# A three-stage kernel (attention, dense layer, eight experts): the third token block is loaded at item 74, the raw weight pieces 4 to 7 use two buffers, and the logits of three blocks come one step later

## The chip, the cores and the metric

The kernel runs on one core of a Trainium2 chip (trn2). The metric is the device time of one launch in microseconds (us), lower is better. Before the change three runs gave 1095.99, 1098.74 and 1099.82 us, with a median of 1098.74 us.

## The reference

Three layers follow one another on 2304 tokens with 512 features (4 batches of 576):

```
scores = q k^T / 8 + bias(positions)          # 4 batches, 8 heads, 576 x 576, head size 64
x = softmax(scores) v                         # -> (2304, 512)
h = x @ w_in                                  # 512 -> 2048
y = (h * clip(h + 3, 0, 6) / 6) @ w_out       # 2048 -> 512
e = argmax(y @ w_gate)                        # one of 8 experts per token
out = softmax(y @ w_gate)[e] * sigmoid(y @ w_output_gate)[e] * (relu(y @ w1[e]) @ w2[e])
```

The weights `w_in` and `w_out` come in double precision and are split on the chip into two single-precision parts, so that each product of the dense layer takes three matmuls.

## The kernel before

**Attention** (class `Attn`) works off 80 items in one software-pipelined loop (`emit`, variable `s`). An item is one pair of heads of one half batch and one chunk of 128 or 64 query rows. Finished rows of x are written, transposed, to the DRAM buffer `xT_d` (L380). At fixed items the loop also calls side work of the dense layer (`early`, added to `side[s]`).

**The dense layer** (class `Moe`) takes the tokens in nine blocks (`b` = 0 to 8) of 256 tokens. `x_load(b)` (L638) brings a block from `xT_d`, `x_prep(b)` splits it into a high part (ScalarE copy, L649 or L656) and a low part (VectorE, L650 or L657). A stage `g` is one pair (b, f) of the list `seq`, where f counts 16 slices of the hidden layer: `l1_` issues 12 matmuls into one PSUM bank `ph` (L671), ScalarE makes `r` = relu(ph + 3) (L677), VectorE `t` (L678), ScalarE the high part of `g` (L680), VectorE its low part (L683); three stages later `l2_` issues 6 matmuls with them (L701). The first round of 48 stages works on blocks 0, 1 and 2 together; its first six stages are (0,0), (0,1), (1,0), (1,1), (2,0), (2,1). Stages 0 and 1 are emitted inside the last attention items, stage 2 comes after all of attention.

In the first round the weights are still being converted. There are 32 **raw pieces** p of 512 KB (even p: a slice of `w_in`, odd p: one of `w_out`). `w_load` (L576) brings a piece into a buffer `V0`, `V1` or `V2`, which attention uses for its v values before; `w_a` is a ScalarE copy of half of it (L603), `w_b` a VectorE shift (L606), `w_c` two VectorE operations, the first of which reads the raw piece for the last time (L609, L610), `w_d` a ScalarE copy and a VectorE subtraction (L613, L614). Pieces 0 to 3 are converted during attention. Pieces 4 and 5 are loaded at item 77. From stage 2 on, two stages of three (and 2, 3 and 4 in a row) carry a tick: tick p runs `w_b(p+1)`, `w_d(p)`, `w_a(p+2)` between the operations of `l1_`, and then `w_c(p+1)`, which also issues the next loads:

```python
self.w_load(p, f"V{(p - 3) % 3}")       # in w_loads(n), for every p up to n
self.conv[p][2](); self.w_loads(p + 4)  # w_c(p)
```

So pieces 6 and 7 are issued behind `w_c(4)`, at item 81, into V0 and V1, and piece 8 behind `w_c(5)`.

Each engine works strictly in the order in which instructions are emitted. All loads and stores named here are issued by SyncE (SP), in one order as well, and SP too stands still at an instruction whose buffer is not free. At stage 2 the code calls `x_load(2)`, `x_prep(2)` and `w_a(5)` ahead of the stage's own work. Block 2's rows go to the buffer `e4`, which belongs to attention's softmax until the end; its two parts go to spare columns of the bias buffers.

Four PSUM banks (m0 to m3) are handed out in turn (`mix`); when block 2's sums begin (l2 of stage 4, emitted at stage 7) they take m0 and m1, and two banks are left until stage 50.

**The tail** of a block (`tail(b)`) has six steps: `s_y` copies and stores y, two `s_t` transpose its halves (L724, copied by L725), `s_l` computes the logits from the transposed y (L730), `s_lt` chooses the expert, `s_r` counts positions. For blocks 0 to 2, `s_l` is emitted in the same stage as the second transpose.

The expert layer follows.

Of the kernel before, what the change touches and what calls it, by code (L numbers as in the profile page):

```python
# [510 lines left out]
class Moe(Base):  # L511
# [122 lines left out]
    def x_load(self, b):  # L634
        if b == 0:
            self.x01 = self.tl("K1", [2, 4, 256], name="xr")
        raw = self.x01[:, b] if b < 2 else self.tl("e4", [4, 256], name="xr")
        self.nc.sync.dma_start(raw, self.xT_d[:, :, b * 256:(b + 1) * 256].rearrange("c p t -> p c t"))  # L638
        self.xs[b] = raw

# [491 lines left out]
    def w_loads(self, n):  # L1132
        while self.loaded < min(n, 32):
            p = self.loaded
            self.w_load(p, f"V{(p - 3) % 3}")
            self.loaded += 1

    def w_a(self, p):
# [12 lines left out]
    def w_c(self, p):  # L1151
        if p < 32:
            self.conv[p][2]()
            self.w_loads(p + 4)

    def w_d(self, p):
        self.conv.pop(p)[3](self.nc.vector)
# [4 lines left out]
    def early(self, N):  # L1162

        ex = {}
        add = lambda s, f: ex.setdefault(s, []).append(f)
        self.loaded, self.conv = 4, {}
        add(31, self.setup)
        add(34, self.setup2)
        for p in range(4):
            for k, f in enumerate(self.w_early(p)):  # L1170
                add(36 + 8 * p + k, f)
        gen = self.emit()
        self.first = gen
        add(73, lambda: (self.x_load(0), self.x_load(1)))
        add(N - 3, lambda: self.w_loads(6))
        add(N - 1, lambda: self.w_a(4))
        add(N, lambda: (self.x_prep(0), self.w_b(4)))
        add(N + 1, lambda: (self.w_c(4), next(gen)))
        add(N + 2, lambda: (self.x_prep(1), next(gen)))
        return ex  # L1180

    def emit(self):
# [8 lines left out]
        add = lambda g, f: at.setdefault(g, []).append(f)  # L1191
# [12 lines left out]
        def tails(b, g, steps):  # L1204
            for k, f in zip(steps, tail[b]):
                add(g + k, f)

        tails(0, 48, (1, 2, 3, 3, 4, 5))
        tails(1, 48, (6, 7, 8, 8, 9, 10))
        tails(2, 48, (2, 12, 13, 13, 14, 15))  # L1210
        for b in range(3, NB - 1):
            tails(b, 16 * (b + 1), (2, 4, 5, 6, 7, 9))
        L = 16 * (NB - 1)
# [25 lines left out]
        for g in range(G + 2):  # L1239
            if g < G:  # L1240
                if g == 2:
                    self.x_load(2)
                    self.x_prep(2)
                    self.w_a(5)
                tk = self.tick(ticks[g]) if g in ticks else ()
                self.l1_(*seq[g], between=tk[:3])
                for f in tk[3:]:
                    f()
            while done2[0] < min(G, g + 1 - (3 if g < 49 else 2)):
                self.l2_(*seq[done2[0]])  # L1250
                done2[0] += 1
            for f in at.get(g, []):
                f()
            if g < 2:
                yield
# [126 lines left out]
```

## Time and profile before

| | us |
|---|---|
| median of three runs (lowest, highest) | 1098.74 (1095.99, 1099.82) |
| the profiled execution, its own time | 1101.62 |
| its span in the trace | 1099.9 |
| TensorE (PE) busy | 1050.7 (96%) |
| VectorE (DVE) busy | 617.7 (56%) |
| ScalarE (ACT) busy | 539.5 (49%) |
| GpSimd (POOL) busy | 221.0 (20%) |

Times in the trace count from the start of the span. Attention ends near 386 us, the first round of 48 stages goes on to about 533 us. Busy time of PE is modelled from pipelined matmuls, so a PE that is shown busy all the time can still be paced by another engine. PEclk is the granted TensorE clock as a share of 2.4 GHz; 0.50 is 1.2 GHz. In brackets behind a row stands the idle time of the engine just before it and what ended it.

### The profile page before, as it was taken

The numbers are of one execution on the slowest core, as the hardware profiler recorded it, in microseconds if no ns is written. First come the engines' busy times: TensorE is split into PE (matmuls) and PEld (weight loads), VectorE is DVE, ScalarE is ACT, GpSimd is POOL, SyncE is SP. The second block draws the span as 40 slices with busy tenths as digits, with TensorE's granted clock in tenths as the row PEclk, the third lists the DMA queues.
The fourth block names the chain that finished last, engine by engine and source line by source line (L and its number), as shares of the span: only waits on it lengthen the run. The fifth ranks groups of instructions, "written<-read, shape, count | busy, mean of one in ns | idle before, by whom it ended". The sixth has DMA issues, their size and how long they took to land. (4 is left out here: it accounts for less than half of the span.)

```text
span 1099.9 us, 20984 instructions
## 1 busy us (share of the span) xinstructions
PE 1050.7 (96%) x7637; PEld 818.7 (74%) x7637; DVE 617.7 (56%) x1554; ACT 539.5 (49%) x1198; POOL 221.0 (20%) x273
## 2 busy tenths in 40 slices
PE   5999999999999979999999999999999989999996
PEld 2355556767777769988788888898887868777774
DVE  4887865667776757776454443436355624345320
ACT  4678777667776644554333333333343123354421
POOL 0132323434444300000010000001311243221111
PEclk9999999999999989999999999999999989999998
DMA  7555481323232143431102010110421265677841
GB/s 233 173 192 171 155 281 50 107 77 97 76 95 75 52 127 113 124 126 58 58 21 39 1 39 1 39 39 2 136 77 33 56 234 209 236 291 278 330 160 38
DMA packets 62192, 129.19 MB, mean 117 GB/s; under 512 B 13820, under 2 KB 35708, under 8 KB 59264
## 3 DMA queue, kind: packets, MB, share of 16 engines
q1 hardware_dynamic: 57424, 117.69, 32.3%
q0 software_dynamic: 4512, 9.49, 3.0%
q8 instruction: 62, 1.02, 0.4%
q10 hardware_dynamic: 144, 0.59, 0.3%
q14 instruction: 50, 0.41, 0.2%
HBM read 164.08 MB, written 14.65 MB: 163 GB/s over the span
## 5 line engine op out<-in xcount | busy, mean ns | idle before, releaser
L701 PE MATMUL acc<-wp,g 128*128 128x512 f32 x864 | 227.3, 398 | 2.1 <-issue 1.7
L671 PE MATMUL ph<-xh,wp 128*128 128x256 f32 x1024 | 207.3, 285 | 1.4 <-ACT y L714 1.2
L701 PEld LDWEIGHTS acc<-wp,g 128*128 128x128 f32 x864 | 154.4, 190 | 29.4 <-issue 2.1
L345 POOL TENSOR_SCALAR e<-e,st 128x576 f32<-128x576 f32 (+1 forms) x160 | 126.2, 801 | 246.0 <-DVE st L343 177.0
L671 PEld LDWEIGHTS ph<-xh,wp 128*128 128x128 f32 x1024 | 167.0, 189 | 11.0 <-issue 3.7
L328 DVE CUSTOM_DVE_ANT_0 e<-sc,bias 128x576 f32<-128x576 f32 (+1 forms) x160 | 116.4, 751 | 63.6 <-PE sc L325 60.9
L671 PE MATMUL ph<-xl,wp 128*128 128x256 f32 x512 | 144.6, 282 | 0.7 <-issue 0.4
L677 ACT ACTIVATE r<-ph,small 128x256 f32<-128x256 f32 x144 | 67.4, 468 | 128.8 <-PE ph L671 124.3
L336 ACT ACTIVATE e<-e,st 128x576 f32<-128x576 f32 (+1 forms) x160 | 123.0, 776 | 0.0
L678 DVE SCALAR_TENSOR_TENSOR t<-r,ph 128x256 f32<-128x256 f32 x144 | 60.3, 419 | 109.8 <-ACT r L677 109.7
L680 ACT ACTIVATE g<-t 128x256 fp32r<-128x256 f32 x144 | 60.2, 418 | 115.0 <-DVE t L678 114.0
L1024 PE MATMUL peh<-ws,xt 128*128 128x512 f32 x408 | 102.7, 405 | 5.1 <-PEq L1334 5.0
L325 PE MATMUL sc<-K,q 64*128 64x288 f32 (+1 forms) x640 | 103.0, 432 | 0.1
L358 PE MATMUL pt<-cst,e 128*128 128x128 f32 (+1 forms) x720 | 97.5, 268 | 2.9 <-ACT eT L361 1.8
L671 PEld LDWEIGHTS ph<-xl,wp 128*128 128x128 f32 x512 | 97.0, 189 | 4.1 <-DVE xl L657 0.5
L358 PEld LDWEIGHTS pt<-cst,e 128*128 128x128 f32 (+1 forms) x720 | 75.8, 141 | 31.7 <-issue 14.1
L775 POOL DMA_INDIRECT tab_d<-small x18 | 18.2, 1008 | 387.6 <-DVE small L773 353.0
L1024 PEld LDWEIGHTS peh<-ws,xt 128*128 128x128 f32 x408 | 76.9, 192 | 23.1 <-issue 5.7
L683 DVE SCALAR_TENSOR_TENSOR g<-t,g 128x256 fp32r<-128x256 f32 x144 | 61.1, 424 | 56.1 <-ACT g L680 56.1
L1052 PE MATMUL peo<-ws,ehh 128*128 128x512 f32 x272 | 86.1, 398 | 0.0
L373 PEld LDWEIGHTS po<-eT,V 128*64 128x64 f32 x1280 | 64.0, 138 | 24.8 <-issue 17.4
L373 PE MATMUL po<-eT,V 128*64 128x128 f32 (+1 forms) x1280 | 81.9, 271 | 0.0
(215 smaller groups left out, 1454.5 us busy)
## 6 DMA issues: line engine op xcount, KB each, us to landing
er<-in_we SPq DMA_DIRECT2D x46, 1024.0 KB
er<-in_we SPq DMA_DIRECT2D x86, 512.0 KB
xb<-in_xb SPq DMA_DIRECT2D x38, 512.0 KB
wraw<-in_wf SPq DMA_DIRECT2D x32, 512.0 KB
cv<-in_xb SPq DMA_DIRECT2D x11, 512.0 KB
K<-in_kT SPq DMA_DIRECT2D x8, 576.0 KB
xr<-xT_d SPq DMA_DIRECT2D x9, 512.0 KB
y_d<-y SPq DMA_DIRECT2D x18, 256.0 KB
```

The costliest lines, as they stand in the source:

```text
L325: nc.tensor.matmul(self.sc[i][:R, n, :288], q[d, pr, :], self.kv[u][d, pr, n * 288:(n + 1) * 288], start=True, stop=True, tile_position=(6 ...
L328: nc.vector.tensor_tensor_reduce(out=e[:R, j, :].rearrange("p (n s) -> p n s", n=2), in0=self.sc[j][:R, :, :288], in1=self.bias[c][:R, 4 * ...
L336: self.nc.scalar.activation(e[:R, j, :], e[:R, j, :], AF.Exp, scale=-1.0, bias=st[:R, j:j + 1], accum_out=st[:R, 4 + j:5 + j])
L345: nc.gpsimd.tensor_scalar(e[:R, j, :], e[:R, j, :], st[:R, 6 + j:7 + j], 1.0, op0=ALU.mult, op1=ALU.mult)
L358: nc.tensor.transpose(pt[:, i, :R], src[3 * gi + i], self.ident[:R, :R])
L373: nc.tensor.matmul(po[64 * j:64 * j + 64, :], vm[:, 2 * pr + j, kb, :], eT[:, 2 * kb + j, :], start=kb == 0, stop=False, tile_position=(0, ...
L671: nc.tensor.matmul(ph, w, x[c], start=n == 0, stop=n == 11)
L677: nc.scalar.activation(r, ph, AF.Relu, bias=self.three)
L683: nc.vector.scalar_tensor_tensor(g[:, 1], t, 1.0 / 6.0, g[:, 0].bitcast(F32), op0=ALU.mult, op1=ALU.subtract)
L701: nc.tensor.matmul(acc[t], x, w, start=f == 0 and i == 0, stop=f == 15 and i == 2)
L1024: nc.tensor.matmul(ph[:, n, :], a, w, start=c == 0 and i == 0, stop=c == 3 and i == 2)
L1052: nc.tensor.matmul(d["po"], a, w, start=f == 0 and i == 0, stop=f == 7 and i == 2)
```

## The change

The load of block 2 moves from stage 2 to item 73 (counted from 0), behind the loads of blocks 0 and 1, and goes to the buffer `cv`, whose last user before is raw piece 3 (items 60 to 64). Raw pieces 4 to 7 use V1, V2, V1, V2. `w_c(4)` and `w_c(5)` issue loads up to piece 6 and piece 7 instead of 7 and 8; from `w_c(6)` on the rule is the old one. The tails of blocks 0 to 2 are spread so that `s_l` comes one stage behind the second transpose; the tail of block 1 so begins one stage later, block 2's transposes too.

```diff
-        raw = self.x01[:, b] if b < 2 else self.tl("e4", [4, 256], name="xr")
+        raw = self.x01[:, b] if b < 2 else self.tl("cv" if b == 2 else "e4", [4, 256], name="xr")
...
-            self.w_load(p, f"V{(p - 3) % 3}")
+            self.w_load(p, f"V{({4: 1, 5: 2, 6: 1, 7: 2}.get(p, (p - 8) % 3))}")
...
-            self.w_loads(p + 4)
+            self.w_loads(p + (3 if p < 6 else 4))
...
-        add(73, lambda: (self.x_load(0), self.x_load(1)))
+        add(73, lambda: [self.x_load(b) for b in range(3)])
...
-        tails(0, 48, (1, 2, 3, 3, 4, 5))
-        tails(1, 48, (6, 7, 8, 8, 9, 10))
-        tails(2, 48, (2, 12, 13, 13, 14, 15))
+        tails(0, 48, (1, 2, 3, 4, 5, 6))
+        tails(1, 48, (7, 8, 9, 10, 11, 12))
+        tails(2, 48, (2, 13, 14, 15, 16, 17))
...
                 if g == 2:
-                    self.x_load(2)
                     self.x_prep(2)
                     self.w_a(5)
```

On SP, from item 73 to stage 2, the order before was this (`xr` with L638 are the block loads, `wraw` with L576 the raw pieces 4, 5, 6 and 7, `xT_d` with L380 the stores of attention):

```order
L638 DMA xr_4267<-xT_d 128x4x256 x2
L380 DMA xT_d<-xo_988_4246 128x2x128
L380 DMA xT_d<-xo_1009_4339 128x2x64
L576 DMA wraw_4446<-in_wf 128x1024
L576 DMA wraw_4448<-in_wf 128x1024
L380 DMA xT_d<-xo_1028_4427 128x2x128
L380 DMA xT_d<-xo_1049_4519 128x2x128
L576 DMA wraw_4625<-in_wf 128x1024
L576 DMA wraw_4627<-in_wf 128x1024
L380 DMA xT_d<-xo_1069_4606 128x2x128
L380 DMA xT_d<-xo_1092_4716 128x2x128
L638 DMA xr_4735<-xT_d 128x4x256
```

With the change the same stretch of SP reads so (the raw pieces are 4, 5, 6 and, last, 7):

```order
L638 DMA xr_4267<-xT_d 128x4x256 x2
L638 DMA xr_4270<-xT_d 128x4x256
L380 DMA xT_d<-xo_988_4246 128x2x128
L380 DMA xT_d<-xo_1010_4341 128x2x64
L576 DMA wraw_4448<-in_wf 128x1024
L576 DMA wraw_4450<-in_wf 128x1024
L380 DMA xT_d<-xo_1029_4429 128x2x128
L380 DMA xT_d<-xo_1050_4521 128x2x128
L576 DMA wraw_4627<-in_wf 128x1024
L380 DMA xT_d<-xo_1070_4608 128x2x128
L380 DMA xT_d<-xo_1092_4716 128x2x128
L576 DMA wraw_4776<-in_wf 128x1024
```

The load of block 2 has moved ahead of six stores and four raw loads, and piece 7 from ahead of the last two stores to behind them.

On PE, at the second transpose of block 0's tail (`py` is its result, `pl` the logits, `ph` and `acc` belong to the stages), the order before was this:

```order
L671 MATMUL ph_6320<-xh_6134,wp_4773 128x256
L701 MATMUL acc_6300<-wp_3714,g_6257 128x512 x6
L724 MATMUL py_6346<-cst,y_6275 128x128 x4
L730 MATMUL pl_6352<-yT_6307,small_2291 32x256 x4
L671 MATMUL ph_6358<-xh_6134,wp_4737 128x256
```

With the change it reads so:

```order
L724 MATMUL py_6346<-cst,y_6275 128x128 x4
L671 MATMUL ph_6352<-xh_6134,wp_4735 128x256
L671 MATMUL ph_6352<-xl_6135,wp_4735 128x256
L671 MATMUL ph_6352<-xh_6134,wp_4735 128x256 x2
L671 MATMUL ph_6352<-xl_6135,wp_4735 128x256
L671 MATMUL ph_6352<-xh_6134,wp_4735 128x256 x2
L671 MATMUL ph_6352<-xl_6135,wp_4735 128x256
L671 MATMUL ph_6352<-xh_6134,wp_4735 128x256 x2
L671 MATMUL ph_6352<-xl_6135,wp_4735 128x256
L671 MATMUL ph_6352<-xh_6134,wp_4735 128x256
L701 MATMUL acc_6300<-wp_4542,g_6295 128x512 x6
L730 MATMUL pl_6378<-yT_6307,small_2291 32x256 x4
```

A whole stage of 18 matmuls now stands between the transposes and the logits; blocks 1 and 2 read alike.

## Rows read from the trace of the kernel before

**Rows 1.** Busy time by stretch: us, busy (instructions) per engine, PEclk, DMA share, GB/s

```profile
390.00:400.00 10.00, 6.27 (x24) 5.01 (x23) 4.89 (x10) 4.10 (x9) 0.00 (x0) 0.66 0.32 107
...
410.00:420.00 10.00, 7.82 (x41) 6.96 (x42) 6.27 (x14) 3.94 (x9) 0.00 (x0) 0.83 0.36 105
...
420.00:535.00 115.00, 115.00 (x730) 102.91 (x729) 82.70 (x171) 56.99 (x126) 0.00 (x0) 1.00 0.30 94
535.00:580.00 45.00, 41.30 (x288) 35.13 (x287) 21.78 (x75) 15.30 (x35) 4.05 (x4) 1.00 0.15 42
```

**Rows 2.** Timeline of SP, 340 to 440 us: start, duration, engine, line, operation

```profile
346.86 1.14 SPq L638 DMA_DIRECT2D xr<-xT_d  x2
...
386.09 0.82 SPq L576 DMA_DIRECT2D wraw<-in_wf  x2
...
387.95 0.55 SPq L638 DMA_DIRECT2D xr<-xT_d  x1
```

**Rows 3.** Timeline of ACT, 386 to 406 us

```profile
386.50 0.27 ACT L378 COPY xo<-po 128x128 f32<-128x128 f32 x1 [1.34 <-PE po L375]
393.61 1.14 ACT L649 CAST wp<-xr 128x512 fp32r<-128x512 f32 x2 [6.84 <-DMA xr<-xT_d]
...
400.68 0.67 ACT L603 ACTIVATE cvc<-wraw 128x512 f32<-128x512 f32 x1
401.25 0.46 ACT L677 ACTIVATE r<-ph,small 128x256 f32<-128x256 f32 x1
...
404.37 0.67 ACT L603 ACTIVATE cva<-wraw 128x512 f32<-128x512 f32 x1
```

**Rows 4.** Timeline of DVE, 386 to 430 us and, the last row, 505 to 515 us

```profile
394.26 1.29 DVE L650 TENSOR_TENSOR wp<-xr,wp 128x512 fp32r<-128x512 f32 x2 [8.70 <-ACT wp L649]
...
398.07 0.69 DVE L609 SCALAR_TENSOR_TENSOR cvd<-wraw,cvd 128x512 int32<-128x512 int32 x1
...
401.75 0.69 DVE L609 SCALAR_TENSOR_TENSOR cvb<-wraw,cvb 128x512 int32<-128x512 int32 x1
...
403.09 0.41 DVE L678 SCALAR_TENSOR_TENSOR t<-r,ph 128x256 f32<-128x256 f32 x1
...
406.76 0.41 DVE L678 SCALAR_TENSOR_TENSOR t<-r,ph 128x256 f32<-128x256 f32 x1
...
411.71 0.42 DVE L678 SCALAR_TENSOR_TENSOR t<-r,ph 128x256 f32<-128x256 f32 x1
...
418.82 0.42 DVE L678 SCALAR_TENSOR_TENSOR t<-r,ph 128x256 f32<-128x256 f32 x1 [2.10 <-ACT r L677]
...
427.45 0.42 DVE L678 SCALAR_TENSOR_TENSOR t<-r,ph 128x256 f32<-128x256 f32 x1
...
513.78 0.42 DVE L678 SCALAR_TENSOR_TENSOR t<-r,ph 128x256 f32<-128x256 f32 x1
```

**Rows 5.** Timeline of PE, 386 to 420 us

```profile
394.28 3.44 PE L671 MATMUL ph<-wp,wp 128*128 128x256 f32 x12 [3.58 <-ACT wp L649]
...
412.18 2.10 PE L671 MATMUL ph<-wp,wp 128*128 128x256 f32 x12 [2.72 <-DVE t L678]
...
416.64 0.28 PE L671 MATMUL ph<-xh,wp 128*128 128x256 f32 x1
...
419.45 0.28 PE L671 MATMUL ph<-xh,wp 128*128 128x256 f32 x1
```

**Rows 6.** Timeline of all engines, 276 to 281 us: one early raw load and its use

```profile
275.85 0.42 SPq L576 DMA_DIRECT2D wraw<-in_wf  x1
...
279.92 0.67 ACT L603 ACTIVATE cva<-wraw 128x512 f32<-128x512 f32 x1 [0.95 <-DMA wraw<-in_wf]
```

**Rows 7.** Timeline of PE, 536 to 582 us: the logits of blocks 0, 1 and 2

```profile
543.01 0.64 PE L730 MATMUL pl<-yT,small 128*32 128x256 f32 x8 [0.78 <-DVE yT L725]
...
560.09 0.64 PE L730 MATMUL pl<-yT,small 128*32 128x256 f32 x8 [0.87 <-DVE yT L725]
...
577.24 0.64 PE L730 MATMUL pl<-yT,small 128*32 128x256 f32 x8 [0.88 <-DVE yT L725]
```

## The prediction

> **What bounds the kernel now.** I read the busy times by stretch first, to find where PE is not busy, then the timelines of SP, ACT, DVE and PE there. Between 390 and 400 us PE is busy 6.27 of 10 us at a mean clock of 0.66, between 410 and 420 us 7.82 of 10 at 0.83, and between 535 and 580 us 41.30 of 45 [rows 1]. The rest of the first round, 420 to 535 us, shows PE busy 115.00 of 115 us. The reader should not take that for a PE bound: the VectorE operation `t` of stage 12 starts at 427.45 and that of stage 42 at 513.78 [rows 4], so three stages take 86.33 / 10 = 8.63 us, while a stage of PE alone takes 419.45 - 416.64 = 2.81 us [rows 5], three of them 8.43. The first round is paced by the chain that DVE and ACT run through each stage to convert weights. What delays that chain near 390 us delays everything up to 514 us, and PE goes straight on behind it.
>
> The chain starts late. ACT copies out the last attention rows at 386.50 for 0.27 us and then stands for 6.84 us until block 2's rows have landed [rows 3]; its two casts start at 393.61, and DVE's first operation on them at 394.26 after 8.70 us of idle [rows 4]. SP shows why: the load is issued at 387.95, behind two raw pieces at 386.09 [rows 2], which had to wait for V0, attention's last v buffer. PE itself loses 3.58 us at stage 4 [rows 5], but that is less than the chain loses.
>
> A second wait follows from the first. Stage 8 of PE starts at 412.18 after 2.72 us of idle, released by the `t` of stage 7 [rows 5], which runs from 411.71 to 412.13 [rows 4]: with two banks left, stage 8 takes the bank that stage 7 has just filled. Behind that idle time the granted clock is at its lower level, 1.2 GHz, for part of 410 to 420 us [rows 1], the 12 matmuls take 2.10 us, and the `t` of stage 9 at 418.82 comes 2.10 us after DVE was ready for it [rows 4].
>
> **The change, part by part.** *The load of block 2* goes onto SP at item 73, as a third issue behind the two that take 1.14 us together at 346.86 [rows 2]: about 0.6 us of SP, far from anything that waits. Its buffer `cv` was last read in items 60 to 64, so SP does not stand still there, and block 2's tokens (512 to 767) were stored before item 50. It has 40 us to land, and ACT's casts follow the last copy of attention directly: from 393.61 to 386.50 + 0.27 = 386.77. The chain moves forward by **6.84 us**. PE's stages 2 and 3 end before that matters, since PE had finished what it could by 394.28 - 3.58 = 390.70 [rows 5].
>
> *The raw pieces.* Piece 6 goes to V1, free behind `w_c(4)`, several us before V0 is: SP is no longer stopped there, and the piece lands early. Piece 7 is new on the path. It now goes out behind the DVE read of piece 5, which ends at 398.07 + 0.69 = 398.76 [rows 4] and with the shift at 391.92. An early raw load was in use 279.92 - 275.85 = 4.07 us after its issue, with ACT waiting for it [rows 6]; so ACT can start piece 7 at 391.92 + 4.07 = 395.99, where the shifted plan has 400.68 - 6.84 = 393.84 [rows 3]. Behind it in ACT's order stands the relu of stage 4, 401.25 - 400.68 = 0.57 us later and 0.46 long [rows 3]: it ends at 397.02. DVE wants it for the `t` at 403.09 - 6.84 = 396.25 [rows 4]. The chain loses 0.77 us. Piece 8 goes out behind the read of piece 6, ending at 401.75 + 0.69 - 6.84 = 395.60 [rows 4], and can be in use at 399.67; the relu behind it ends 1.03 us later, at 400.70, and the `t` of stage 5 is due at 406.76 - 6.84 + 0.77 = 400.69 [rows 4]. So piece 8 costs nothing more. Piece 9, queued behind piece 8, is used two stages later, and from piece 10 on the distance is the old one. I take **0.8 us back**.
>
> Bounds for that: no loss if a load is usable in 3.3 us; for the upper end I take the longest wait that the trace has near here, block 2's own load with two raw pieces in front, 393.61 - 387.95 = 5.66 us [rows 2, 3]. With it piece 8's relu ends at 395.60 + 5.66 + 1.03 = 402.29 against 399.92 planned, a loss of 2.4. I take the 4.07 because the same kind of transfer, alone, is the nearest row.
>
> The Trainium skill ("DMA: Bandwidth & Descriptors", section "Anatomy of one DMA — SWDGE (gpsimd) path") gives about 2.0 us plus bytes over 436 GB/s, for loads issued by GpSimd; an estimate by that page for 512 KB is 3.2 us, by which the loss would be nil and the time 0.8 us lower. The row of this case is 0.9 us longer, and I go by the row.
>
> *The second wait* stays. PE's operations before stage 8 and stage 8 itself are both released by the chain, so they move together, the idle time stays near 2.7 us and I expect the lower clock behind it as before, with the same 2.1 us on the `t` of stage 9. If the clock did not fall, up to 2.1 us more would be won; that goes into the range, not into the sum.
>
> *The tails.* For blocks 0, 1 and 2 PE waits 0.78, 0.87 and 0.88 us for DVE's copy of the second transpose before the logits [rows 7]; that is 2.53 of the 3.70 us of PE idle between 535 and 580 us [rows 1]. A stage of 2.81 us now stands between, longer than the wait. The matmuls are the same ones; DVE has no conversion there any more (21.78 of 45 us busy [rows 1]), and buffers of the tails are taken again many stages later. **2.5 us** won; the bounds are 0 and 2.53.
>
> **The sum.** 6.84 - 0.8 + 2.5 = 8.5 us. The profiled execution took 1101.62 us by itself, so it would take 1093.1. The median of the runs is 1098.74, 2.88 us under it; I give **1090.2 us** for the median.
>
> **The rivals.**
>
> *The load waits eat most of it.* Pieces 7, 8 and 9 come in a burst and ACT stands in order at each. By the upper end the chain gains 6.84 - 2.4 = 4.4 us; if part of the tails' gain is lost too (say 1 of 2.5), 5.9 us, which is 1092.8; if all of it, 4.4 us and 1094.3. For it: block 2's load took 5.66 us with two others in front. Against it: piece 7 has no other load in front, piece 8 is ahead of 9 on the queue. Chance 0.13.
>
> *No change.* The chain's start is not what holds PE, because some other wait of the same length stands behind the load, and only the tails' 2.5 us are won: 1096.2 us. Against it: ACT's 6.84 us are put down to the load alone, and its inputs otherwise, PE's stage 2, are finished before 390.70. Chance 0.06.
>
> *Slower.* The raw loads run late for good, not for one piece. In the old distance a load has from 398.76 to 404.37, 5.61 us, until ACT wants it [rows 3, 4], and the relu behind it has 403.09 - 401.71 = 1.38 us to spare; beyond 7.0 us each of the 24 loads from piece 8 on delays the chain that paces the whole round. At 7.6 us a load, 24 x 0.6 = 14.4 us are lost against 8.5 + 0.8 = 9.3 won: 1103.8 us. It decides from a load time of about 7.4 us. Against it: 4.07 and 5.66 us, and the order of SP, which is the old one from piece 9 on. Chance 0.03.
>
> **How the numbers follow.** The forecast has 0.78; its own range runs from 1087.3 (no loss to loads and no fall of the clock: 6.84 + 2.1 + 2.5 = 11.4 us) to 1092. The stated range reaches down to 1086.5, since the three runs lie up to 2.75 us under their median, and up to 1094.0, most of the first rival. A measurement of this kernel can tell about 0.3%, 3.3 us, from no change: faster takes the forecast and the first rival, 0.91; same 0.06; slower 0.03.
>
> **What would show it.** SP: three block loads in a row near 347 us, one raw load near 379, none between it and about 392. ACT: the casts at about 386.8 with no wait on a load, then a wait of some 2 us for piece 7 and of 1 to 2 us for piece 8. DVE: `t` of stage 4 near 397.0, that of stage 12 near 421.4. PE: no wait at stage 4, still some 2.7 us at stage 8 with the lower clock behind it, and no wait for the logits of blocks 0 to 2. I am wrong if the stage-12 `t` has moved by less than 4 us, if ACT waits 4 us or more for raw pieces, or if the waits at the logits are still there or stand at another tail operation.

## The result and the profile after

| | before | after |
|---|---|---|
| median, us (lowest to highest, 5 runs each, same chip) | 1098.74 (1095.99 to 1100.15) | 1088.31 (1085.26 to 1088.48) |
| ratio of the two, 95% interval | | 0.9902 [0.9881, 0.9922] |
| the profiled execution, its own time | 1101.62 | 1088.37 |
| its span | 1099.9 | 1086.6 |

The changed kernel is faster by 10.4 us in the median and by 13.25 us between the two profiled executions. The forecast was 8.5 us. The time lies in the range that was given, near the predicted 1090.2. One execution of E6 below (1156.88 us at a granted clock of 0.849) belongs to a slower state of the core and is left out of the median there. The first part of the page of the changed kernel shows where to look: PE has fewer busy microseconds than before (1050.7), though every matmul is still there (x7637 in both). The rows by stretch below fit with fewer of them at the lower clock.

```profile
PE 1044.1 (96%) x7637; PEld 814.8 (75%) x7637; DVE 617.9 (57%) x1554; ACT 538.7 (50%) x1198; POOL 220.7 (20%) x273
```

The busy times by stretch of the changed kernel, with the columns of [rows 1]:

```profile
390.00:400.00 10.00, 9.72 (x63) 8.67 (x63) 7.65 (x16) 4.33 (x10) 0.00 (x0) 1.00 0.56 172
400.00:410.00 10.00, 6.98 (x26) 5.49 (x25) 7.23 (x15) 4.55 (x10) 0.00 (x0) 0.67 0.44 143
410.00:420.00 10.00, 10.00 (x67) 9.18 (x67) 6.40 (x13) 4.36 (x10) 0.00 (x0) 0.99 0.20 57
...
535.00:580.00 45.00, 45.00 (x317) 38.33 (x316) 24.48 (x92) 15.56 (x38) 4.21 (x4) 1.00 0.08 23
```

The hole between 390 and 400 us is gone (6.27 us busy before, 9.72 now, clock 0.66 and now 1.00). The second hole has moved forward, from 410 to 420 into 400 to 410 us, with a clock of 0.67. From 535 to 580 us PE no longer idles (41.30 before).

SP, which issues the loads, in the changed kernel between 340 and 440 us (start, duration, line, operation):

```profile
345.56 1.69 SPq L638 DMA_DIRECT2D xr<-xT_d  x3
...
377.47 0.34 SPq L576 DMA_DIRECT2D wraw<-in_wf  x1
379.93 5.93 SPq L380 DMA_DIRECT2D xT_d<-xo  x2
390.60 45.92 SPq L576 DMA_DIRECT2D wraw<-in_wf  x12
```

Three block loads go out in a row. One raw piece (6) goes out at 377.47, and none after it until piece 7 at 390.60. ACT in the same stretch:

```profile
385.21 0.27 ACT L378 COPY xo<-po 128x128 f32<-128x128 f32 x1 [1.34 <-PE po L375]
385.37 1.14 ACT L649 CAST wp<-xr 128x512 fp32r<-128x512 f32 x2
...
394.30 0.68 ACT L603 ACTIVATE cvc<-wraw 128x512 f32<-128x512 f32 x1 [1.76 <-DMA wraw<-in_wf]
396.66 0.68 ACT L603 ACTIVATE cva<-wraw 128x512 f32<-128x512 f32 x1
```

The casts follow the last copy of attention with no wait, where 6.84 us stood before [rows 3]. Piece 7 is waited for, 1.76 us; it is used 394.30 - 390.60 = 3.70 us after its issue. Piece 8, at 396.66, is not waited for. DVE, the `t` of stages 4, 8, 9, 12 and 42:

```profile
395.37 0.42 DVE L678 SCALAR_TENSOR_TENSOR t<-r,ph 128x256 f32<-128x256 f32 x1 [0.44 <-ACT r L677]
...
408.01 0.42 DVE L678 SCALAR_TENSOR_TENSOR t<-r,ph 128x256 f32<-128x256 f32 x1 [0.24 <-ACT r L677]
...
412.13 0.42 DVE L678 SCALAR_TENSOR_TENSOR t<-r,ph 128x256 f32<-128x256 f32 x1 [2.80 <-ACT r L677]
...
420.76 0.42 DVE L678 SCALAR_TENSOR_TENSOR t<-r,ph 128x256 f32<-128x256 f32 x1
...
507.08 0.42 DVE L678 SCALAR_TENSOR_TENSOR t<-r,ph 128x256 f32<-128x256 f32 x1
```

The wait for piece 7 reaches DVE as 0.44 us. The wait at stage 9 is 2.80 us (2.10 before [rows 4]). PE at stage 8, and the logits of blocks 0 to 2:

```profile
404.48 2.93 PE L671 MATMUL ph<-wp,wp 128*128 128x256 f32 x12 [2.71 <-DVE t L678]
407.20 2.76 PE L701 MATMUL acc<-wp,g 128*128 128x512 f32 x6
...
538.27 0.64 PE L730 MATMUL pl<-yT,small 128*32 128x256 f32 x8
...
557.22 0.64 PE L730 MATMUL pl<-yT,small 128*32 128x256 f32 x8
...
573.40 0.64 PE L730 MATMUL pl<-yT,small 128*32 128x256 f32 x8
```

Stage 8 waits as long as before (2.72, [rows 5]) but its 12 matmuls took longer, 2.93 instead of 2.10 us. That is not a mark of the change: in E9, another execution of the kernel before, they take 2.93 too. The logits wait for nothing.

**Where the 13.25 us are.** Four landmarks that both traces have split the difference: the last copy of attention (ACT, L378), the `t` of stage 12, block 3's first transpose (PE, L724) and the first matmul of the experts (PE, L1024).

| stretch | before | after | difference |
|---|---|---|---|
| start to last copy | 386.50 | 385.21 | -1.29 |
| last copy to `t` of stage 12 | 40.95 | 35.55 | -5.40 |
| that to block 3's transpose | 170.54 | 167.75 | -2.79 |
| that to the first expert matmul | 217.69 | 214.69 | -3.00 |

The third row ends at these two rows of PE, first before and then after:

```profile
597.99 0.60 PE L724 MATMUL py<-cst,y 128*128 128x128 f32 x4
```

```profile
588.51 0.60 PE L724 MATMUL py<-cst,y 128*128 128x128 f32 x4
```

What is left of the 13.25, some 0.8 us, comes later. The change acts directly on the middle two rows, -8.19 us together. The others are outside the sum of the prediction. The first can't be told from scatter: over the twelve profiles of this study the last copy of attention lies between 381.42 and 386.50 us, and among the earliest is one of a kernel whose loads are those of before (E2, 382.73).

### The profile page after: what moved, and what is told of

Read it like the earlier page. It is cut to its first block, busy times and chain, and to the rows that moved or that the text cites. A ratio compares the mean times of both kernels' runs of the same rounds, so it can differ in the third digit from the quotient of the medians.

```text
span 1086.6 us, 20980 instructions
## 1 busy us (share of the span) xinstructions
PE 1044.1 (96%) x7637; PEld 814.8 (75%) x7637; DVE 617.9 (57%) x1554; ACT 538.7 (50%) x1198; POOL 220.7 (20%) x273
## 5 line engine op out<-in xcount | busy, mean ns | idle before, releaser
L1024 PE MATMUL peh<-ws,xt 128*128 128x512 f32 x408 | 102.7, 405 | 4.5 <-PEq L1333 4.4
L1024 PEld LDWEIGHTS peh<-ws,xt 128*128 128x128 f32 x408 | 76.9, 192 | 22.5 <-issue 5.0
```

What stands on the lines that cost most here:

```text
L1024: nc.tensor.matmul(ph[:, n, :], a, w, start=c == 0 and i == 0, stop=c == 3 and i == 2)
```

## The experiments

Several kernels of one job ran on the same chip and share the runs of the kernel before there. Medians of different jobs differ by some us, so a local reading is used beside them: the time of a landmark after the last copy of attention, in the profiled execution. All of them in one table, with `t 2` for the `t` of stage 2 and so on, and B3 for block 3's first transpose:

| kernel | t 2 | t 4 | t 8 | t 9 | t 12 | B3 | median (before, same job) | ratio [95%] |
|---|---|---|---|---|---|---|---|---|
| before | 9.22 | 16.59 | 28.90 | 32.32 | 40.95 | 211.49 | 1098.74 | |
| changed | 2.27 | 10.16 | 22.80 | 26.92 | 35.55 | 203.30 | 1088.31 (1098.74) | 0.9902 [0.9881, 0.9922] |
| E1 without the tails | 2.29 | 10.16 | 22.79 | 25.69 | 34.32 | 204.84 | 1089.02 (1095.28) | 0.9945 [0.9926, 0.9965] |
| E2 tails only | 9.18 | 16.55 | 28.85 | 32.26 | 40.89 | 208.61 | 1091.32 (1095.28) | 0.9968 [0.9952, 0.9984] |
| E3 old buffers for raw pieces | 2.30 | 9.67 | 21.98 | 25.41 | 34.04 | 201.76 | 1084.27 (1095.28) | 0.9913 [0.9889, 0.9936] |
| E4 other bank at stage 8 | 2.29 | 10.14 | 22.46 | 23.72 | 32.35 | 200.07 | 1084.84 (1095.28) | 0.9908 [0.9888, 0.9929] |
| E5 changed kernel again | 2.28 | 10.26 | 22.89 | 25.86 | 34.49 | 202.22 | 1082.99 (1093.39) | 0.9903 [0.9882, 0.9923] |
| E6 PE kept busy | 2.28 | 10.23 | 22.54 | 24.41 | 33.05 | 200.79 | 1083.08 (1093.39) | 0.9912 [0.988, 0.9944] |
| E7 shorter chain | 2.30 | 8.74 | 18.88 | 21.48 | 29.91 | 197.19 | 1079.06 (1093.39) | 0.9869 [0.9848, 0.989] |
| E8 three together | 2.27 | 8.18 | 18.32 | 20.22 | 28.70 | 195.99 | 1077.76 (1093.39) | 0.9858 [0.9834, 0.9882] |
| E9 before again | 9.14 | 16.51 | 29.15 | 32.06 | 40.69 | 211.24 | 1096.72 (1095.13) | 0.9998 [0.9973, 1.0022] |
| E10 raw buffers only | 6.71 | 15.32 | 27.63 | 29.50 | 38.14 | 208.69 | 1094.11 (1095.13) | 0.9981 [0.9952, 1.0009] |

Two reruns of one program show what the table can tell: the changed kernel's `t 9` is 26.92 and 25.86 in two executions, B3 203.30 and 202.22, and before's B3 211.49 and 211.24. Local differences under about 1 us behind stage 8 say nothing.

### E1: the change without the tails

```diff
-        tails(0, 48, (1, 2, 3, 4, 5, 6))
-        tails(1, 48, (7, 8, 9, 10, 11, 12))
-        tails(2, 48, (2, 13, 14, 15, 16, 17))
+        tails(0, 48, (1, 2, 3, 3, 4, 5))
+        tails(1, 48, (6, 7, 8, 8, 9, 10))
+        tails(2, 48, (2, 12, 13, 13, 14, 15))
```

> The change without the spread of the tails: block 2 loaded at item 74 and pieces 4 to 7 in two buffers, the logits of blocks 0 to 2 back in the stage of the second transpose. Theory (the two parts act apart and add up): from the last copy of the attention rows to the t of stage 12 the trace needs 35.5 us as with the whole change (before 40.95), the three waits at the logits are back with 0.8 to 0.9 us each, and the time is 2.5 to 2.8 us above the whole change, about 1091 us. Rival (part of what the medians show beyond the two parts, 10.4 - 5.4 - 2.8 = 2.2 us, hangs on the tails): 5 us above the whole change, about 1093. Rival (the tails give nothing): 1088.

The median is 6.26 us under that of before in its job. Up to stage 8 the readings are those of the changed kernel within 0.02 us, and PE's waits at the logits are back:

```profile
534.28 0.64 PE L730 MATMUL pl<-yT,small 128*32 128x256 f32 x8 [0.78 <-DVE yT L725]
...
551.36 0.64 PE L730 MATMUL pl<-yT,small 128*32 128x256 f32 x8 [0.88 <-DVE yT L725]
...
568.52 0.64 PE L730 MATMUL pl<-yT,small 128*32 128x256 f32 x8 [0.88 <-DVE yT L725]
```

B3 lies 6.65 us before that of the kernel before. So the early loads are the larger part, and they work without the tails. By the time alone the tails' share is not settled: by the ratios this kernel is 0.43%, 4.7 us, slower than the whole change, nearer to the first rival's 5 us than to the 2.5 to 2.8 expected, and two intervals of some 4 us each do not decide between them. At B3 it is 1.54 us behind the changed kernel and 2.62 behind its rerun E5.

### E2: the tails alone

Made on the kernel before, with the new `tails` lines and nothing else.

> The kernel before with the spread of the tails alone. Theory: the waits at the logits of blocks 0 to 2 go (0.78 + 0.87 + 0.88 = 2.53 us), everything up to 530 us stays (40.9 us from the last attention copy to the t of stage 12), the time is about 1096 us, 2.5 to 2.8 us under before. Rival (the tails alone also save the issue gaps of PE near 783 us, 2 us and some clock): 1093 to 1094. Rival (the wait moves to another tail operation): 1098.7 and a new wait of 0.8 us in the tails.

The median is 3.96 us lower than before's in the job (interval 1.8 to 5.3 us by the ratio, which takes in the theory's 2.5 to 2.8 and the first rival's 5). B3 moves by 2.88 us, from 211.49 to 208.61, and up to stage 12 all is as before within 0.06 us. The waits at the logits are gone:

```profile
541.10 0.64 PE L730 MATMUL pl<-yT,small 128*32 128x256 f32 x8
560.04 0.64 PE L730 MATMUL pl<-yT,small 128*32 128x256 f32 x8
```

The parts add: -6.65 and -2.88 at B3 make -9.53; the changed kernel has -8.19 and, in E5, -9.27 there, and the spread between these two is that of `t 9`. The sum of the two ratios' gains, 0.55% and 0.32%, is 9.5 us.

### E3: the raw pieces in their old buffers

```diff
-            self.w_load(p, f"V{({4: 1, 5: 2, 6: 1, 7: 2}.get(p, (p - 8) % 3))}")
+            self.w_load(p, f"V{(p - 3) % 3}")
...
-            self.w_loads(p + (3 if p < 6 else 4))
+            self.w_loads(p + 4)
```

> The whole change, but raw pieces 4 to 7 keep the old three buffers and the old distance (pieces 6 and 7 issued behind the last reader of V0). Theory (two buffers cost the chain a wait of ACT for piece 7, 1.76 us long, of which 0.5 us reaches DVE; the early block load gives the rest): no wait for piece 7; piece 6 goes out near 384.8 us and can be in use 4 us later, at 388.9, just when ACT wants it at 388.8; from the last attention copy to the t of stage 12 about 35.0 to 35.5 us and a time within 0.6 us of the whole change, 1087.7 to 1088.3. Rival (the two buffers are what makes the early load work, because piece 6 is late otherwise): ACT waits 2 us or more for piece 6 or 7, and the time is 1 to 3 us above the whole change.

SP issues pieces 6 and 7 together, as soon as V0 comes free, and ACT uses piece 7 with no wait. The first view is SP's, the second ACT's:

```profile
382.41 0.82 SPq L576 DMA_DIRECT2D wraw<-in_wf  x2
```

```profile
386.41 0.69 ACT L603 ACTIVATE cva<-wraw 128x512 f32<-128x512 f32 x1
...
390.09 0.67 ACT L603 ACTIVATE cvc<-wraw 128x512 f32<-128x512 f32 x1
```

The `t` of stage 4 comes 9.67 us after the last copy instead of 10.16, and that of stage 8 at 21.98 instead of 22.80. So what the new buffers of the raw pieces cost, once block 2 is loaded early, is some 0.5 to 0.8 us; they give nothing back in that case. That is local; in the ratio (0.9913) it can't be seen.

### E4: stage 8 takes the other bank

With two banks left, the order in which they are handed out is turned round, so stage 8 takes the one that is free earlier.

```diff
-            own, Base.banks = sorted(Base.banks)[:2], sorted(Base.banks)[2:]
+            own, Base.banks = sorted(Base.banks)[:2], sorted(Base.banks)[:1:-1]
```

> The whole change, and when the sums of block 2 take two banks, the two that are left are handed out in the other order, so that stage 8 takes the one that stage 4 used and not the one of stage 7. Theory (the wait of 2.71 us at stage 8 and the lower clock behind it hold the chain up: the t of stages 8 and 9 wait 0.24 and 2.80 us for the relu): the wait at stage 8 goes, the clock stays at 1.00, the t of stage 9 comes some 3.0 us earlier, and as DVE paces the round up to stage 42 the whole time falls by 3 us, to about 1085. Rival (PE catches up in the round anyway, as PE alone needs less per stage): the wait goes but the t of stage 42 is where it was, 1088. Rival (the wait only moves to stage 9 or 10): the idle time of PE between 390 and 420 us stays at 3.3 us, 1087 to 1088.

The busy times from 390 to 420 us, first of the changed kernel and then of this one:

```profile
390.00:420.00 30.00, 26.70 (x152) 23.34 (x152) 21.28 (x43) 13.24 (x29) 0.00 (x0) 0.89 0.40 124
```

```profile
390.00:420.00 30.00, 28.87 (x180) 24.85 (x179) 23.30 (x49) 15.44 (x35) 0.00 (x0) 1.00 0.44 141
```

The clock no longer falls. The wait of 2.71 us is gone. Besides 0.56 us in the l2 of stage 4, which the changed kernel has too (0.58), what is left is 0.58 us at a later stage:

```profile
408.81 0.39 PE L671 MATMUL ph<-xh,wp 128*128 128x256 f32 x1 [0.58 <-DVE t L678]
```

The `t` of stage 9 comes at 23.72, 3.20 us before the changed kernel's and 2.14 before that of its rerun, and B3 follows (200.07 against 203.30 and 202.22). The ratio, 0.9908, is the changed kernel's: a gain of 2 to 3 us is not to be seen across two jobs whose intervals are 4 us wide. It is shown locally and not in the time.

### E5: the changed kernel again

No edit.

> The changed kernel itself once more, beside the other runs of this call, as the mark for them. From the last attention copy to the t of stage 8 the trace should need 22.8 us as before, to the t of stage 9 between 25.7 and 26.9 us, as the two runs with the same code up to there did, depending on where the lower clock falls.

It has 0.9903 once more, 10.4 us. `t 9` is 25.86 here: the same wait at stage 8, and 1.06 us less behind it.

### E6: PE kept busy before stage 8

Twenty matmuls, whose result nobody reads, are added to PE ahead of stage 8's first matmul. The wait on the bank stays.

```diff
+                if g == 8:
+                    spare = self.bank("m3", [256], "spare")
+                    wi = self.pieces[0]
+                    for _ in range(20):
+                        self.nc.tensor.matmul(spare, wi[:, 0:128], self.xs[1][0][0], start=True, stop=True)
```

> The changed kernel with 20 extra matmuls of 128x256 into an unused bank ahead of stage 8 (some 2.3 us of PE work that nothing reads), so that PE works through most of the 2.71 us in which stage 8 waits for its bank. Theory (not the wait but the lower clock behind it holds up the chain): the clock stays at 1.00, stage 8 starts as late as without the extra work, its 12 matmuls take 1.6 and not 2.9 us, the t of stage 8 does not wait and that of stage 9 comes 2 to 3 us earlier, 24 us behind the last attention copy; the time falls by 1.5 to 3 us although PE does more. Rival (the wait itself is the cost): the t of stage 9 stays at 25.7 us or more and the time does not fall, or rises by the extra work.

PE's timeline shows the filler in the hole, and stage 8 released by the same `t`:

```profile
398.78 2.52 PE L1249 MATMUL spare<-xh,wp 128*128 128x256 f32 x20
401.66 1.69 PE L671 MATMUL ph<-wp,wp 128*128 128x256 f32 x12 [0.36 <-DVE t L678]
```

The `t` of stage 9 on DVE, and the busy times:

```profile
406.74 0.42 DVE L678 SCALAR_TENSOR_TENSOR t<-r,ph 128x256 f32<-128x256 f32 x1 [0.55 <-ACT r L677]
```

```profile
400.00:410.00 10.00, 9.64 (x66) 8.68 (x65) 7.55 (x16) 4.86 (x10) 0.00 (x0) 1.00 0.34 105
```

Stage 8 starts 19.33 us after the last copy (401.66 - 382.33), against 404.48 - 385.21 = 19.27 in the changed kernel. It starts no earlier. But its 12 matmuls take 1.69 instead of 2.93 us, and the `t` of stage 9 comes at 24.41 instead of 26.92 or 25.86. So most of the local cost is the clock behind the wait, 1.45 to 2.51 us at `t 9`. What the wait costs by itself is the rest to E4, which has neither: 24.41 - 23.72 = 0.69 us, less than two executions of one kernel can differ by. In the time it can't be seen: 1083.08 against 1082.99 of E5 in the same job, where 1.5 to 3 us less were expected.

### E7: a shorter tick on DVE

The first DVE operation of `w_c`, the last that reads the raw piece, goes right behind `w_b`, where DVE otherwise waits for ACT's copy in `w_d`; the next load is issued behind it. The two operations of `w_c` become steps of their own, 4 and 5 of a piece's list.

```diff
-        return (lambda: self.w_b(p + 1), lambda: self.w_d(p), lambda: self.w_a(p + 2), lambda: self.w_c(p + 1)) if p < 32 else ()
+        def b_():
+            self.w_b(p + 1)
+            if p + 1 < 32:
+                self.conv[p + 1][4]()
+                self.w_loads(p + 1 + (3 if p + 1 < 6 else 4))
+
+        def c_():
+            if p + 1 < 32:
+                self.conv[p + 1][5]()
+
+        return b_, lambda: self.w_d(p), lambda: self.w_a(p + 2), c_
```

> The changed kernel with one operation moved on DVE: the first operation of w_c, 0.69 us, stands ahead of the subtraction of w_d, where DVE waits 0.66 us for ACT in every tick, and the loads behind it go out that much earlier. Theory (the round is paced by the chain of DVE and ACT, 8.63 us for three stages, and PE alone needs 8.43): a tick takes about 3.0 instead of 3.68 us on DVE, three stages then fall to PE's 8.43, the wait at stage 8 shrinks to some 0.2 us with no lower clock, and the time falls by 6 us (waits and clock near stage 8) plus 2 us (33 stages at 2.81 instead of 2.88), to 8 us under the changed kernel. Rival (PE paces the round at 2.88 us a stage by itself): the wait near stage 8 goes, the pace stays, 5 to 6 us. Rival (ACT becomes the bound, or the raw loads, which are wanted earlier): waits for raw pieces at several ticks, less than 4 us.

The median falls by 1082.99 - 1079.06 = 3.9 us, and B3 by 202.22 - 197.19 = 5.0 us, where 8 us were expected. Late raw pieces are not the reason: between 380 and 530 us ACT waits for one piece alone, 1.03 us for piece 7. The wait at stage 8 is not gone, but it is short and the 12 matmuls behind it take 1.68 us:

```profile
399.85 1.68 PE L677 MATMUL ph<-wp,wp 128*128 128x256 f32 x12 [0.98 <-DVE t L684]
```

The lines of this kernel are six higher than those of the changed one. DVE's next `t` comes sooner, and from 420 us on it is DVE that waits for PE (through ACT's relu):

```profile
421.76 0.42 DVE L684 SCALAR_TENSOR_TENSOR t<-r,ph 128x256 f32<-128x256 f32 x1 [1.15 <-ACT r L683]
...
430.17 0.42 DVE L684 SCALAR_TENSOR_TENSOR t<-r,ph 128x256 f32<-128x256 f32 x1 [1.17 <-ACT r L683]
```

Three stages take 430.17 - 421.76 = 8.41 us here, PE's own pace, where the changed kernel's takes 8.63 and its `t` waits for nothing. What was won lies ahead of stage 12 (34.49 - 29.91 = 4.6 us of the 5.0), and 22.89 - 18.88 = 4.0 of it ahead of the `t` of stage 8. Behind it 0.4 us more are won, where ten times 8.63 - 8.41 would be 2.2. The reason stands in PE's rows of the changed kernel, the l2 of some stages early and late in the round:

```profile
436.60 1.57 PE L701 MATMUL acc<-wp,g 128*128 128x512 f32 x6
439.42 1.54 PE L701 MATMUL acc<-wp,g 128*128 128x512 f32 x6
442.21 1.55 PE L701 MATMUL acc<-wp,g 128*128 128x512 f32 x6
...
484.75 1.55 PE L701 MATMUL acc<-wp,g 128*128 128x512 f32 x6
...
493.38 1.57 PE L701 MATMUL acc<-wp,g 128*128 128x512 f32 x6
```

Early a stage follows the last after 2.81 us, late three take 493.38 - 484.75 = 8.63 us. Behind stage 8 PE is in arrears, works them off at its own pace, and has caught up with DVE only late in the round. Over the whole round the two limits lie within half a microsecond of each other.

### E8: E7, E4 and E3 together

E7's tick with the old load rule (`w_loads(p + 1 + 4)` and `w_loads(p + 4)`), E4's order of banks and E3's old buffers.

> The same with the old buffers and distances for pieces 4 to 7 and with the other order of the two banks. Theory (what these two gave by themselves, 0.5 and 3.2 us, is the same waits that the moved operation takes away): within 1 us of the run with the moved operation alone, at most 1.5 us faster. Rival (the gains add): 3 to 4 us faster than that run. Rival (piece 6 is now late, since the chain wants it earlier): 1 us or more slower.

It is the fastest kernel here: 1077.76 us, 1.3 us under E7 in the same job, 15.6 us under before and 5.2 under the changed kernel. Its difference to E7 is within the intervals, and 1.2 us at B3, as the theory has it; the 3 to 4 us of the rival, by which the gains of E3 and E4 would add, are not seen. Against the changed kernel it is clear of the noise: its slowest execution took 1078.57 us, the fastest of E5 1082.7.

### E9: the kernel before again

No edit.

> The kernel before itself once more. The local readings should repeat: 40.9 us from the last attention copy to the t of stage 12, 6.8 us of ACT waiting for block 2, 2.7 us of PE waiting at stage 8, three waits at the logits. Open is whether the issue gaps of PE near 783 us (2.0 us with a lower clock behind them, in the one trace of before) belong to this kernel: if they do, they are there again and the stretch from block 3's first transpose to the first expert matmul takes 217.7 us; if that execution was a chance one, it takes 214.7 us as in all runs of the changed forms.

The ratio to itself is 0.9998. The local readings repeat: ACT's wait for block 2 is 6.77 us, PE's at stage 8 2.72, those at the logits 0.78, 0.87 and 0.88. Only the 12 matmuls behind the wait take 2.93 us here, and 2.10 in the first profile [rows 5]:

```profile
411.25 2.93 PE L671 MATMUL ph<-wp,wp 128*128 128x256 f32 x12 [2.72 <-DVE t L678]
```

It was run for the 3.00 us between B3 and the first expert matmul, which no part of the change explains. The stretch takes 216.34 us here, between the two values expected, against 217.69 in the first profile of this kernel, 214.7 in the changed kernel and E1 to E4, 213.5 in E5 to E8 and 215.57 in E10. PE's rows of the first profile of before there:

```profile
782.58 0.28 PE L671 MATMUL ph<-xl,wp 128*128 128x256 f32 x1 [0.35 <-issue]
...
783.98 0.39 PE L701 MATMUL acc<-wp,g 128*128 128x512 f32 x1 [1.01 <-issue]
784.71 0.39 PE L701 MATMUL acc<-wp,g 128*128 128x512 f32 x1 [0.34 <-issue]
785.40 1.87 PE L701 MATMUL acc<-wp,g 128*128 128x512 f32 x4 [0.31 <-issue]
```

These are 2.01 us in which PE waits for nothing that the profile shows, and matmuls behind them are at the lower clock (four in 1.87 us, six in 1.56 elsewhere). E9 has 1.56 us of such gaps near 782 us, E10 0.75, the changed kernel 0.16. E2 with the old loads and E1 with the old tails have 0.32 and 0.26. Put in order by the time at which B3 starts in the trace, the gaps are 2.01 us (597.99), 1.56 (596.87), 0.75 (593.90) and 0.32 (591.34), and at most 0.31 in the eight traces where it starts before 590 us. So the later a kernel gets there, the larger they are. That is an order over twelve traces; what makes the gaps was not tried and stays open.

### E10: the raw buffers alone

Made on the kernel before: the new map of buffers and `w_loads(p + (3 if p < 6 else 4))`, block 2 still loaded at stage 2.

> The kernel before with only the buffers and distances of raw pieces 4 to 7 changed; block 2 is still loaded at stage 2, the tails are the old ones. Theory (of the 5.66 us from that load's issue to its use part is the two raw pieces in front): the load goes out behind the last two stores with nothing before it, about 1 us earlier, and is in use some 4.1 us after its issue, so that ACT's wait is 4.5 to 5 us instead of 6.84 and the t of stage 12 comes 1.5 to 2.5 us earlier (38.5 to 39.4 us behind the last attention copy); the time falls by 1.5 to 2.5 us. Rival (the load takes as long by itself): ACT waits 6 us or more and the time is that of before. Rival (the wait for piece 7 is added): the t of stage 12 at 40 us or more.

SP's row of block 2's load and ACT's rows show both effects:

```profile
385.96 0.41 SPq L638 DMA_DIRECT2D xr<-xT_d  x1
```

```profile
389.81 1.14 ACT L649 CAST wp<-xr 128x512 fp32r<-128x512 f32 x2 [4.34 <-DMA xr<-xT_d]
...
399.48 0.66 ACT L603 ACTIVATE cvc<-wraw 128x512 f32<-128x512 f32 x1 [2.50 <-DMA wraw<-in_wf]
```

Block 2's load, issued at 385.96, is used 3.85 us later instead of 5.66. So 2.5 us of the 6.84 were owed to the two raw pieces in front of it: 0.7 because the load goes out sooner after the last copy, 1.8 because it is in use sooner. Piece 7 then takes 1.2 us of that back by stage 4, so 1.3 are left. At `t 12` it is 2.8 against the first profile of before, but the rest comes from elsewhere: here PE waits earlier, the slow matmuls are those of the l2 of stage 4, and the 12 of stage 8 are fast again:

```profile
404.68 2.93 PE L701 MATMUL acc<-wp,g 128*128 128x512 f32 x6 [3.47 <-DVE t L678]
409.63 1.68 PE L671 MATMUL ph<-wp,wp 128*128 128x256 f32 x12 [2.02 <-DVE t L678]
```

The time doesn't tell (0.9981, and its interval holds 1).

## Why the prediction was right, and where not

The forecast case happened, and the landmarks stand near where they were put: the `t` of stage 12 at 420.76 (predicted 421.4), that of stage 4 at 395.37 (397.0), with attention ending 1.29 us sooner in this execution. Counted from the last copy they are 35.55 us where 34.9 were forecast, and 10.16 where 10.5 were. Of the sum, -8.5 us were expected, and -8.19 (E5 against E9: -9.0) were measured up to block 3's first transpose. That -8.19 comes so near is in part luck: the block load, piece 7 and the tails gave 0.1, 0.25 and 0.3 us more than forecast, and in this execution the clock took 1.0 us back. Step by step:

- *Block 2's load, 6.84 us.* Shown. The `t` of stage 2 comes 6.95 us sooner after the last copy, the casts start even 0.11 us before the copy's end. The rival "no change", that another wait stands behind this one, is out.
- *Piece 7, 0.8 us back.* Right in kind, 0.5 in size: from `t 2` to `t 4` there are 7.89 us instead of 7.37. The load was in use after 3.70 us, not the 4.07 of [rows 6]. By the formula of the Trainium skill ("DMA: Bandwidth & Descriptors", section "Anatomy of one DMA — SWDGE (gpsimd) path"), which is for loads issued by GpSimd, an estimate for 512 KB is 3.2 us. The three loads measured here with nothing in front, issued by SP, were in use after 3.70, 3.85 and 4.07 us, all longer, so the measurement stands.
- *Piece 8.* A wait of 1 to 2 us on ACT was announced and there was none: it was in use at 396.66, before the predicted 399.67. Nothing hung on it in the sum. The rivals that rested on longer loads (5.66 us and more) are out.
- *The second wait.* It stayed, 2.71 us, with the lower clock behind it, as forecast. It does not follow from the first wait, as the working has it: the first is gone and the second stands, and E4 shows that the order of the banks makes it. **The step that did not hold is the one that left the clock's price as it was**, "the same 2.1 us on the `t` of stage 9". In this execution that `t` waited 2.80 us, the stretch from `t 4` to `t 9` took 16.76 us instead of 15.73, and the gain at stage 12 was 5.40 instead of 6.04. But the change is not what raised the price: the same stretch takes 15.60 us in E5 and 15.55 in E9, 15.53 to 15.74 in E1 to E3, and from E9 to E5 the gain at stage 12 is 6.20. The price belongs to the execution, with the wait the same within 0.01 us, and one trace can't give it to better than 1 us. E6 shows that most of it is the clock's (1.45 to 2.51 us with the wait kept and the clock granted in full).
- *The tails, 2.5 us.* Shown by E1 and E2, 2.79 to 2.88 us at B3, a little over the sum of the three waits of 2.53.
- *The chain paces the round.* That a shift near 390 us reaches the end held: -5.40 us at stage 12 are -5.42 at stage 48, and DVE's `t` goes from stage 12 to 42 in 86.32 us as before (86.33). But the reading that the chain paces PE all the way to 514 us was too simple. PE goes at its own 2.81 us a stage for a good half of the round and meets the chain late. The shift was carried on because both moved together, PE being held at stage 8 by the same chain; E7, which shortened the chain alone, got 0.4 us behind stage 12 instead of 2.2.
- *What was not in the sum.* The median moved by 10.4 us in both jobs. The forecast's 8.5 us lie at the very edge of the intervals (8.6 to 13.1 us here, 8.4 to 12.9 in E5's job), so some 2 us are not accounted for by the sum. The gaps of PE near 783 us are a candidate: 2.01 and 1.56 us in the two profiles of before, 0.16 and none in the two of the changed kernel. In the order of the twelve traces the kernels that get there several us sooner have less of them, so a change that moves everything forward may save them by that alone. It is not shown that this change does.

## What to carry to other kernels

A small load that is the first thing an engine needs in a new phase should be issued as soon as a buffer for it can be found, and ahead of bulk loads on its queue: here the early load gave 6.9 us at its first use, and of that 2.5 us were the loads in front alone. Once it is early, look again at the rules that were made around it: the two-buffer rule for raw pieces cost 0.5 to 0.8 us locally, and the kernel without it was no slower. When PE is shown busy without a break, compare the spacing of its stages with that of the engine that feeds it, at several places: where the two differ PE is working off arrears, and a shorter chain gives less than the difference of the paces.

## What the runs showed of the hardware

- A wait of 2.7 us of PE was followed by the lower of the two clock levels, and the 12 matmuls behind it took 2.10 us in one execution of the kernel before and 2.93 in another; with PE kept busy by other matmuls through the same wait the clock was granted in full and they took 1.69. In E10 six matmuls behind a wait of 3.47 us took 2.93 us (1.55 elsewhere), and twelve behind the next wait, of 2.02 us, took 1.68.
- A 512 KB load issued by SP was in use 3.70, 3.85 and 4.07 us after issue when nothing was in front, and after 5.66 us behind two loads of the same size.
- PE showed gaps of up to 1.01 us each, 2.01 us together, without a releaser, in the first profile of before, and 1.56 us in the same stretch of the second; in the first the matmuls behind them ran at the lower clock (a mean of 0.79 granted from 782 to 790 us). They were the larger the later the kernel came to that stretch.
